# Attention followed by a gated MLP on one Trainium2 core: every second high half of batches three and four on ScalarE, five slots for the probabilities' halves, one bias tile kept in SBUF instead of two

## The chip, the cores and the metric

The kernel runs on one core of a Trainium2 chip. The metric is the device time of one execution in microseconds (us), and less is better. A profile of one execution comes with it; its span runs from the first to the last instruction of the core.

## The reference

Four batches of 576 tokens go through attention with 8 heads of 64, whose scores get a bias that a small MLP makes from relative positions and that all batches share. The 2304 x 512 result then goes through two matrix products with a gated activation between them.

```python
scores = scale * np.matmul(q, k.transpose(0, 1, 3, 2))          # (4, 8, 576, 576)
x = (psi_rel / psi_i)[..., None]                                # from log1p of positions
h = np.maximum(x @ w1 + b1, 0.0)                                # hidden 32
bias = h @ w2                                                   # one value per head
scores = scores + bias.transpose(2, 0, 1)[None, :, :, :]
attn = softmax(scores)                                          # max subtracted, 1e-9 in the divisor
y = np.matmul(attn, v)                                          # back to (2304, 512)
h = y @ w_in                                                    # 512 -> 2048
g = h * np.clip(h + 3.0, 0.0, 6.0) / 6.0
out = g @ w_out                                                 # 2048 -> 512
```

## The kernel before

Numbers that need more than 16 bits are carried as a high and a low float16 half, and a product is summed from three half products. In the code batches count from 0, so that batches three and four of the title are `b` = 2 and `b` = 3.

**Tiles of the attention.** `tiles` lists 144 tiles in order: 4 batches x 4 pairs of heads (`p`) x 9 tiles (`t`) of 128 rows of scores x 576 columns. One tile goes through a fixed pipeline, one stage behind the other:

- `qk_step` (L465): scores on TensorE into a PSUM bank `s_ps`.
- `soft_max` (L477): VectorE adds the bias tile `bt`, keeps the row minimum of the negated sum in `sm` and writes the sum to `bt`.
- `soft_exp` (L485): ScalarE takes the exponential in place and sums the rows.
- `soft_norm` (L491, L499): VectorE takes the reciprocal of the row sum. Then `high_part` writes the **high half** of the scaled probabilities into the first half of a new tile `hl` (128 x 1152 float16): on GpSimd (POOL) at L104, or on ScalarE (ACT) at L110. `hl_mode` reads which one from the configuration: `hl0` for batch one, `hl1` for batch two, `hl` for the batches after, as a string of letters (P POOL, A ACT) that is indexed by the tile's number.
- `soft_low` (L127): VectorE computes the **low half** from `bt` and the high half.
- `soft_turn` (L555): SyncE (SP) issues a DMA that transposes the whole `hl` into the tile `at`. After that the slot of `hl` is free.
- `pv_step` (L630): TensorE multiplies nine transposed chunks with the values' halves; `x_high` (L647, ACT) and `x_low` (L127, VectorE) store the result as halves in `x`.

Most tiles of batch one ("direct", letter F in the configuration) skip the halves and are transposed on TensorE in float32 (L538), so that 118 of the 144 tiles use `hl`.

**Slots.** `hl` comes from a pool of three slots. `bias_out` uses the same slots under the name `bo` (L816): in the first 150 us it evacuates 36 groups of the bias table from PSUM on ACT and SP writes them to DRAM (L818). `load_bias` (L419, L424) later reads bias tiles back from DRAM through SP's queue, two DMAs a tile, each tile being used by two tiles of scores. The bias tiles that `KEEP` lists by (pair, tile) are read once in batch one into a constant tile `kb` and never again.

**The MLP.** `ffn(b, u)` is a generator for half a batch: L705 makes hidden rows `h_ps`, L695, L688, L682 and L684 turn them into the halves `g` (ACT, VectorE, ACT, POOL), L731 multiplies with the second weights and L741 evacuates to `ot`. Its steps are handed out between tiles of the attention by the loop over `n` at the end, so that TensorE has MLP work while a tile waits. What the attention does not take along is done after it.

**The order** of instructions on each engine is not the order of the code: a scheduler places them by priorities and by a timeline that it models for itself, and which includes waits for slots. So a change of a pool's size can move instructions in places that do not use the pool.

Of the kernel before, what the change touches and what calls it, by code (L numbers as in the profile page):

```python
# [24 lines left out]
NG = S // 16  # L25
CQ = 2.0 ** -25
VC = 5 * 128
CFG = {'bw': 0, 'z0': 'ADDD', 'gz': 6, 'zeng': 'AD', 'evac': 'A', 'sg': 'P', 'wm1': 'A', 'wm2': 'A', 'hl1': 'AP', 'ql1': 'PP', 'ql': 'PP', 'gl0': 'PP', 'gl': 'PP', 'hl': 'P', 'vm': 'A', 'g0': 16, 'rwi': 3.0, 'rw0': 0.2, 'rw1': 1.3, 'rb': 1.4, 'rb1': 1.0, 'ro': 3.0, 'rf0': 1.2, 'rf': 1.78, 'rf1': 1.0, 'ch': 1, 'pa': [0, 0, 20], 'la': 6, 'z1': 'AD', 'gz2': 28, 'gq': 2, 'wu': 8, 'act': '', 'tv': 'AAD', 'pf': [0, 0, 0], 'pw': 0, 'po': 0, 'pb': 0, 'sw': 4, 'nb': 0, 'nb1': 0, 'f': 'FFFFFFDD', 'hl0': 'P'}
F64_BIAS = 2.0 ** -112
F64_MAX = float(np.uint32(0x0FEFFFFF).view(np.float32))  # L30

# [2 lines left out]
def attention_moe_kernel(  # L34
# [17 lines left out]
    nc = tc.nc  # L52
    cfg = CFG
    tc.cur_priority = 10000
# [10 lines left out]
    st_p = ctx.enter_context(tc.tile_pool(name="st", bufs=2))  # L65
    v_p = ctx.enter_context(tc.tile_pool(name="v", bufs=2))
    b_p = ctx.enter_context(tc.tile_pool(name="b", bufs=4))
    hl_p = ctx.enter_context(tc.tile_pool(name="hl", bufs=3))
    sm_p = ctx.enter_context(tc.tile_pool(name="sm", bufs=6))
    dr_p = ctx.enter_context(tc.tile_pool(name="dr", bufs=1, space=bass.MemoryType.DRAM))  # L70
    pools = {}
# [332 lines left out]

    bt_t = {}

    KEEP = [(1, 1), (3, 1)]
    kept = {}

    def load_bias(b, p, i):  # L410
        out = b_p.tile([128, 2 * S], F32, tag="bt", name="bt")
        t = out
        if (p, i) in KEEP:
            if b:
# [713 lines left out]
```

## Time and profile before

| | |
|---|---|
| Median of 3 runs | 767.28 us (765.88 to 770.45) |
| Profiled execution, own time | 768.73 us |
| its span | 766.8 us |
| its mean granted TensorE clock | 0.973 |

The span is the profile's own time axis. 768.73 - 766.8 = 1.9 us of the profiled execution's time lie around the span. TensorE's rows are PE (matmuls) and PEld (weight loads); DVE is VectorE, SPq the queue of SyncE. In a row of a timeline the bracket gives the idle time of the engine before the instruction and what ended it.

### The profile page before, as it was taken

The page shows a single profiled execution, that of the slowest core. Times are in us where ns is not written, and L with a number is a line of the kernel's source. Part 1 is how long each engine was busy: PE and PEld are TensorE (multiplying, and loading weights), DVE is VectorE, ACT ScalarE, POOL GpSimd, SP SyncE. Part 2 cuts the span into 40 slices and gives each one's busy share as a digit, 9 for nine tenths or more (in the row PEclk, how much of TensorE's full clock was granted, in tenths as well). Part 3 has the DMA queues.
Part 4 walks back from the last instruction along what each step waited for, and adds up shares of the span by engine and source line. Part 5 has one row for each costly group of instructions (what it writes and reads, how often), then busy time and mean ns, then how long its engine had stood idle before and what let it go on. Part 6 is the DMA issues. An engine that isn't in the chain of part 4 may idle for free.

```text
span 766.8 us, 15078 instructions
## 1 busy us (share of the span) xinstructions
PE 693.5 (90%) x5340; PEld 482.9 (63%) x5340; DVE 509.3 (66%) x1307; ACT 451.8 (59%) x911; POOL 293.8 (38%) x348
## 2 busy tenths in 40 slices
PE   6667788899888888999789999999999999999998
PEld 2223334566567765666576777667877766588775
DVE  7997999998888558876678568746866672030210
ACT  5897999778567358755566366436743661161530
POOL 4111111127564127524576267616652460041320
PEclk9877899999999999999999999999999999999999
DMA  8999767387999999999999998899788642000000
GB/s 256 363 304 285 217 182 233 115 250 219 254 233 224 197 219 215 237 219 259 180 247 224 220 253 150 212 166 220 161 168 172 116 77 64 11 7 22 8 10 27
DMA packets 179275, 137.98 MB, mean 180 GB/s; under 512 B 145920, under 2 KB 152064, under 8 KB 179200
## 3 DMA queue, kind: packets, MB, share of 16 engines
q1 hardware_dynamic: 174592, 132.30, 72.8%
q10 hardware_dynamic: 4608, 4.72, 2.4%
q8 instruction: 42, 0.69, 0.4%
q14 instruction: 33, 0.27, 0.1%
HBM read 84.78 MB, written 15.34 MB: 131 GB/s over the span
## 4 chain that ended last, share of the span: by engine, by line
PE 39%; DMA 13%; DVE 10%; issue 6%; POOL 4%; ACT 3%; SPq 2%; POOLq 0%; ACTq 0%; DVEq 0%
PE o_ps L731 17%; PE h_ps L705 14%; DMA at<-hl 7%; PE pv_ps L630 5%; PE s_ps L465 3%; DVE hl L127 3%; DMA va<-in_vp_dram 3%; DVE bt L477 2%; POOL hl L104 2%; DMA bt<-bias 2%; POOL kl L368 1%; DVE t L688 1%; SPq L419 1%; ACT bt L485 1%; DVE vparts L158 1%
## 5 line engine op out<-in xcount | busy, mean ns | idle before, releaser
L731 PE MATMUL o_ps<-g,wo 128*128 128x256 f16 (+1 forms) x1536 | 227.6, 289 | 5.1 <-ACT ot L741 3.4
L705 PE MATMUL h_ps<-x,wi 128*128 128x256 f16 (+1 forms) x1536 | 218.1, 288 | 7.5 <-DVE t L688 4.7
L731 PEld LDWEIGHTS <-wo 128*128 128x128 f16 x1536 | 146.2, 98 | 59.5 <-issue 7.5
L705 PEld LDWEIGHTS <-wi 128*128 128x128 f16 x1536 | 146.1, 98 | 55.8 <-issue 10.5
L485 ACT ACTIVATE bt<-bt,sm 128x576 f32<-128x576 f32 x144 | 111.1, 771 | 102.0 <-DVE sm L477 87.9
L127 DVE SCALAR_TENSOR_TENSOR hl<-bt,sm,hl 128x576 f16<-128x576 f32 x118 | 120.9, 1029 | 58.9 <-POOL hl L104 51.8
L684 POOL TENSOR_TENSOR g<-t,g 128x256 f16<-128x256 f32 (+1 forms) x128 | 105.4, 832 | 122.0 <-ACT g L682 114.4
L104 POOL TENSOR_SCALAR hl<-bt,sm 128x576 f16<-128x576 f32 x100 | 78.2, 784 | 151.4 <-DMA at<-hl 54.1
L477 DVE CUSTOM_DVE_ANT_0 bt<-s_ps,bt 128x576 f32<-128x576 f32 x128 | 95.1, 748 | 11.0 <-PE s_ps L465 6.2
L688 DVE SCALAR_TENSOR_TENSOR t<-t,t,h_ps 128x320 f32<-128x320 f32 (+1 forms) x112 | 57.2, 513 | 61.5 <-ACT t L695 60.8
L795 PE MATMUL b_ps<-z,w_sb 128*32 128x288 f32 x576 | 67.5, 486 | 28.7 <-ACT z L783 17.9
L682 ACT ACTIVATE g<-t 128x256 f16<-128x256 f32 (+1 forms) x128 | 55.2, 435 | 38.6 <-DVE t L688 38.3
L228 POOL TENSOR_SCALAR w<-w 128x512 f32<-128x512 f32 x32 | 23.0, 718 | 138.6 <-ACT cu L226 118.3
L695 ACT ACTIVATE t<-h_ps,t,hr 128x320 f32<-128x320 f32 (+1 forms) x112 | 65.2, 586 | 18.4 <-PE h_ps L705 12.0
L630 PE MATMUL pv_ps<-at,vh 128*64 128x256 f16 (+1 forms) x468 | 65.7, 296 | 4.8 <-DMA at<-hl 4.6
L795 PEld LDWEIGHTS b_ps<-z,w_sb 128*32 128x32 f32 x576 | 23.6, 121 | 65.8 <-ACT z L783 31.6
L465 PE MATMUL s_ps<-qkh 128*128 128x288 f32 x192 | 53.2, 353 | 7.6 <-DVE sm L477 3.6
L783 ACT ACTIVATE z<-T,bp 128x576 f32<-128x576 f32 x66 | 48.1, 770 | 11.2 <-PE b_ps L795 6.6
L465 PE MATMUL s_ps<-kl,qkh 128*128 128x288 f32 x192 | 50.3, 332 | 0.0
L741 ACT ACTIVATE ot<-o_ps,os 128x256 f32<-128x256 f32 (+1 forms) x32 | 15.8, 494 | 58.2 <-PE o_ps L731 58.1
L630 PEld LDWEIGHTS <-vh 128*64 128x64 f16 x468 | 31.4, 108 | 29.1 <-issue 8.0
L465 PE MATMUL s_ps<-k0t,q0t 128*128 128x288 f32 x144 | 45.6, 443 | 4.3 <-DVE sm L477 2.6
(110 smaller groups left out, 855.2 us busy)
## 6 DMA issues: line engine op xcount, KB each, us to landing
bt<-bias SPq DMA_DIRECT2D x112, 288.0 KB, 4.6
st<-in_qk_dram SPq DMA_DIRECT2D x24, 576.0 KB, 4.7
bias<-bo SPq DMA_DIRECT2D x36, 288.0 KB, 4.6
w<-in_w_in_dram SPq DMA_DIRECT2D x16, 512.0 KB, 7.1
w<-in_w_out_dram SPq DMA_DIRECT2D x16, 512.0 KB, 4.8
vs<-in_vp_dram SPq DMA_DIRECT2D x20, 320.0 KB, 3.7
va<-in_vp_dram SPq DMA_DIRECT2D x16, 320.0 KB, 4.9
bt<-bias SPq DMA_DIRECT2D x32, 144.0 KB, 3.7
```

The costliest lines, as they stand in the source:

```text
L104: nc.gpsimd.tensor_scalar(out=out, in0=full, scalar1=scale, scalar2=1.0, op0=ALU.mult, op1=ALU.mult)
L127: nc.vector.scalar_tensor_tensor(out=out, in0=full, scalar=scale, in1=high, op0=ALU.mult, op1=ALU.subtract)
L465: nc.tensor.matmul(out=ps[:, a, 0:HALF], lhsT=w, rhs=m[:, a * HALF:(a + 1) * HALF], start=(k == 0), stop=(k == len(ops) - 1),)
L477: nc.vector.tensor_tensor_reduce(out=halves(bt), in0=ps, in1=halves(src), op0=ALU.add, op1=ALU.min, scale=-0.125, scalar=3.0e38, accum_out ...
L485: nc.scalar.activation(out=bt, in_=bt, func=AF.Exp, scale=-1.0, bias=sm[:, 0:1], accum_out=sm[:, 1:2])
L630: nc.tensor.matmul(out=ps[64 * s:64 * s + 64, 0:n], lhsT=w[:, 128 * c + 64 * s:128 * c + 64 * s + 64], rhs=at[:, c, s * n:(s + 1) * n], st ...
L684: e.tensor_sub(out=g[:, 1], in0=uu, in1=g[:, 0])
L688: nc.vector.scalar_tensor_tensor(out=t_t[f], in0=t_t[f], scalar=cols(f)[2], in1=h_t.pop(f)[:, 0:n], op0=ALU.min, op1=ALU.mult,)
L695: nc.scalar.activation(out=t_t[f], in_=h_t[f][:, 0:n], func=AF.Relu, scale=cols(f)[0], bias=cols(f)[1],)
L705: nc.tensor.matmul(out=h_t[f][:, 0:n], lhsT=wi[:, a, c, f * 128:(f + 1) * 128], rhs=x[:, e, c], start=(k == 0), stop=(k == 3 * KC - 1),)
L731: nc.tensor.matmul(out=ops[:, 0:n], lhsT=wo[:, a, f, e * 128:(e + 1) * 128], rhs=g_t[f][:, r], start=(f == 0 and a == 0 and r == 0), stop= ...
L795: nc.tensor.matmul(out=pss[a][32 * k:32 * k + 32, 0:HALF], lhsT=w2_sb, rhs=z[:, a * HALF:(a + 1) * HALF],)
```

## The change

Three edits:

- `'hl': 'P'` becomes `'hl': 'AP'`: in batches three and four the high half of tiles with an even number goes to ACT (L110), that of the others stays on POOL (L104). Batch two has had `AP` (`hl1`) before and after.
- The pool of `hl` and `bo` has five slots instead of three.
- `KEEP` loses (3, 1): this bias tile is read from DRAM into `bt` in every batch, like the tiles that were never kept. A kept tile takes 128 x 1152 float32, 4608 bytes a partition, and two slots of `hl` take as much.

```diff
-CFG = {... 'gl': 'PP', 'hl': 'P', 'vm': 'A', ...}
+CFG = {... 'gl': 'PP', 'hl': 'AP', 'vm': 'A', ...}
...
-    hl_p = ctx.enter_context(tc.tile_pool(name="hl", bufs=3))
+    hl_p = ctx.enter_context(tc.tile_pool(name="hl", bufs=5))
...
-    KEEP = [(1, 1), (3, 1)]
+    KEEP = [(1, 1)]
```

What this makes of the order, first on ACT, in batch three, around the evacuations of the MLP's output `ot`. In the kernel before (`bt` the exponential, `tq` a part of the next head's queries, `x` the attention's result):

```order
L741 ACTIVATE ot<-o_ps,os_4404 128x256
L742 DMA out_dram<-ot 128x256
L485 ACTIVATE bt,sm<-bt,sm 128x576
L378 ACTIVATE tq_111<-qkh 128x64
L647 ACTIVATE x<-pv_ps,xr 128x256
L378 ACTIVATE tq_112<-qkh 128x64
L485 ACTIVATE bt,sm<-bt,sm 128x576 x2
```

In the changed kernel, at the same place:

```order
L485 ACTIVATE bt,sm<-bt,sm 128x576 x2
L110 ACTIVATE hl<-bt,sm 128x576
L741 ACTIVATE ot<-o_ps,os_4405 128x256
L647 ACTIVATE x<-pv_ps,xr 128x256
L742 DMA out_dram<-ot 128x256
L485 ACTIVATE bt,sm<-bt,sm 128x576 x2
L741 ACTIVATE ot<-o_ps,os_4405 128x256
L110 ACTIVATE hl<-bt,sm 128x576
```

A high half now stands between the exponentials, once for every two of them; 54 stand on ACT instead of 18 and 64 on POOL instead of 100.

Second, SP's queue at the last pair of heads of batch two. Before (`bias_97` to `bias_105` are the nine parts of the bias table, two for a bias tile):

```order
L419 DMA bt<-bias_97 64x1152
L419 DMA bt<-bias_98 64x1152
L555 DMA_TRANSPOSE at<-hl 128x9x128 x3
L354 DMA st<-in_qk_dram 128x1152
L419 DMA bt<-bias_101 64x1152
```

With the change:

```order
L419 DMA bt<-bias_97 64x1152
L419 DMA bt<-bias_98 64x1152
L555 DMA_TRANSPOSE at<-hl 128x9x128 x2
L419 DMA bt<-bias_99 64x1152
L419 DMA bt<-bias_100 64x1152
L555 DMA_TRANSPOSE at<-hl 128x9x128 x2
```

Two loads of a bias tile stand where none stood; the same holds for batches three and four, six loads in all. On TensorE the order of the 4884 matmuls differs in 634 places, all of them in the first 70% of the order.

## Rows read from the trace of the kernel before

**Rows 1.** Stretches: us, busy us (instructions) of PE PEld DVE ACT POOL, PEclk, DMA share, GB/s.

```profile
0.00:100.00 100.00, 69.52 (x466) 27.94 (x467) 89.73 (x224) 78.53 (x121) 18.59 (x34) 0.83 0.90 284
100.00:200.00 100.00, 88.73 (x668) 56.65 (x668) 92.70 (x283) 84.43 (x163) 31.89 (x38) 1.00 0.69 199
200.00:250.00 50.00, 39.67 (x318) 32.47 (x318) 41.98 (x112) 32.08 (x70) 27.48 (x31) 0.97 1.03 239
250.00:300.00 50.00, 45.94 (x372) 34.56 (x370) 32.18 (x77) 28.45 (x59) 18.19 (x19) 0.97 1.01 206
300.00:350.00 50.00, 45.59 (x334) 30.81 (x331) 38.55 (x100) 33.75 (x69) 22.11 (x24) 1.00 1.14 231
350.00:400.00 50.00, 42.41 (x373) 34.76 (x372) 33.88 (x86) 27.45 (x65) 27.91 (x31) 1.00 1.03 230
400.00:450.00 50.00, 48.57 (x396) 36.62 (x396) 34.11 (x84) 24.12 (x54) 21.64 (x28) 1.00 1.06 224
450.00:700.00 250.00, 249.64 (x1939) 181.59 (x1938) 137.37 (x329) 123.23 (x275) 113.30 (x130) 1.00 0.62 128
```

**Rows 2.** The chain that ended last, 244 to 262 us: start, us, what.

```profile
246.00 7.74 DMA at<-hl
...
253.92 0.76 POOL hl L104
...
254.70 0.83 DVE hl L127
...
255.55 3.25 DMA at<-hl
```

**Rows 3.** Line L555 from 200 to 450 us: who waited for the transposes (us, times).

```profile
  POOL hl L104: 46.5, 12
  ACT hl L110: 13.0, 6
...
DMA to landing us min/median/max: 3.2/4.7/10.0
```

**Rows 4.** TensorE's timeline: matmuls after idle time, start, us, engine, line.

```profile
249.65 0.60 PE L731 MATMUL o_ps<-g,wo 128*128 128x256 f16 x4 [3.44 <-ACT ot L741]
...
261.16 1.03 PE L731 MATMUL o_ps<-g,wo 128*128 128x256 f16 x8 [1.63 <-DVE x L127]
...
306.35 1.41 PE L630 MATMUL pv_ps<-at,vh 128*64 128x320 f16 x18 [1.42 <-DMA at<-hl]
...
367.78 1.41 PE L630 MATMUL pv_ps<-at,vh 128*64 128x320 f16 x18 [3.18 <-DMA at<-hl]
...
381.27 0.37 PE L465 MATMUL s_ps<-qkh 128*128 128x288 f32 x1 [2.37 <-DVE sm L499]
...
387.23 1.03 PE L705 MATMUL h_ps<-x,wi 128*128 128x256 f16 x8 [1.55 <-DVE x L127]
```

**Rows 5.** The tile hl: count, ns min/median/max, first and last start.

```profile
L104 POOL TENSOR_SCALAR hl<-bt,sm x100: 737/744/1427, 181.3 to 636.6; 128x576 f16<-128x576 f32 x100
L110 ACT ACTIVATE hl<-bt,sm x18: 757/775/777, 226.6 to 348.3; 128x576 f16<-128x576 f32 x18
```

**Rows 6.** Timeline from 310 to 313 us: POOL and two low halves.

```profile
310.91 0.82 DVE L127 SCALAR_TENSOR_TENSOR hl<-bt,sm,hl 128x576 f16<-128x576 f32 x1 [1.04 <-ACT hl L110]
...
312.31 0.79 POOL L684 TENSOR_TENSOR g<-t,g 128x320 f16<-128x320 f32 x1
...
312.38 1.34 DVE L127 SCALAR_TENSOR_TENSOR hl<-bt,sm,hl 128x576 f16<-128x576 f32 x1 [0.36 <-POOL hl L104]
```

**Rows 7.** DMA issues: KB each, median us to landing.

```profile
bt<-bias SPq DMA_DIRECT2D x112, 288.0 KB, 4.6
```

**Rows 8.** VectorE's timeline: two readings of the kept bias tile.

```profile
327.84 0.74 DVE L477 CUSTOM_DVE_ANT_0 bt<-s_ps,kb 128x576 f32<-128x576 f32 x1
...
462.08 0.74 DVE L477 CUSTOM_DVE_ANT_0 bt<-s_ps,kb 128x576 f32<-128x576 f32 x1
```

**Rows 9.** ACT's timeline: the one wait of bo for a slot.

```profile
65.37 0.83 ACT L816 ACTIVATE bo<-b_ps,cv_sb,isc 128x576 f32<-128x576 f32 x1 [1.61 <-DMA bias<-bo]
```

More of the change, by code (lines that the diff above doesn't have):

```diff
@@ L27 @@
 VC = 5 * 128
-CFG = {'bw': 0, 'z0': 'ADDD', 'gz': 6, 'zeng': 'AD', 'evac': 'A', 'sg': 'P', 'wm1': 'A', 'wm2': 'A', 'hl1': 'AP', 'ql1': 'PP', 'ql': 'PP', 'gl0': 'PP', 'gl': 'PP', 'hl': 'P', 'vm': 'A', 'g0': 16, 'rwi': 3.0, 'rw0': 0.2, 'rw1': 1.3, 'rb': 1.4, 'rb1': 1.0, 'ro': 3.0, 'rf0': 1.2, 'rf': 1.78, 'rf1': 1.0, 'ch': 1, 'pa': [0, 0, 20], 'la': 6, 'z1': 'AD', 'gz2': 28, 'gq': 2, 'wu': 8, 'act': '', 'tv': 'AAD', 'pf': [0, 0, 0], 'pw': 0, 'po': 0, 'pb': 0, 'sw': 4, 'nb': 0, 'nb1': 0, 'f': 'FFFFFFDD', 'hl0': 'P'}
+CFG = {'bw': 0, 'z0': 'ADDD', 'gz': 6, 'zeng': 'AD', 'evac': 'A', 'sg': 'P', 'wm1': 'A', 'wm2': 'A', 'hl1': 'AP', 'ql1': 'PP', 'ql': 'PP', 'gl0': 'PP', 'gl': 'PP', 'hl': 'AP', 'vm': 'A', 'g0': 16, 'rwi': 3.0, 'rw0': 0.2, 'rw1': 1.3, 'rb': 1.4, 'rb1': 1.0, 'ro': 3.0, 'rf0': 1.2, 'rf': 1.78, 'rf1': 1.0, 'ch': 1, 'pa': [0, 0, 20], 'la': 6, 'z1': 'AD', 'gz2': 28, 'gq': 2, 'wu': 8, 'act': '', 'tv': 'AAD', 'pf': [0, 0, 0], 'pw': 0, 'po': 0, 'pb': 0, 'sw': 4, 'nb': 0, 'nb1': 0, 'f': 'FFFFFFDD', 'hl0': 'P'}
 F64_BIAS = 2.0 ** -112
```

## The prediction, made before the changed kernel had run

> **What bounds the kernel now.** I read stretches first, since shares over the span mix stages. The reader should compare PE's busy time with the length of each stretch [rows 1]. From 450 to 700 us PE is idle for 0.36 us in 250, and what is left after that is MLP work alone: what happens there on ACT, POOL or SP moves nothing, as long as PE's work is the same. Before that PE is idle for 30.5 us in the first 100, 11.3 in the next 100, and 10.3 + 4.1 + 4.4 + 7.6 + 1.4 = 27.8 us between 200 and 450. As PE's work doesn't change, a gain can only come out of these idle times, and out of stretches at the lower clock (0.97 from 200 to 300, 0.83 in the first 100).
>
> From 0 to 200 DVE is busy for 182 of 200 us and ACT for 163: this is the bias table and the preparation of weights, and the pool of `hl` serves it only as `bo`. From 200 to 450 no engine but PE is near full: DVE is busy for 42 of the first 50 us and for 39 and less after, ACT for at most 34, POOL for 28. There the chain of waits is the view to read [rows 2]: a transpose holds a slot for 7.74 us, POOL's next high half starts right after it, DVE's low half follows, the next transpose starts. That is a ring through a pool with too few slots. Line L555's view gives its size [rows 3]: producers of high halves waited 46.5 + 13.0 = 59.5 us for transposes between 200 and 450, 18 times. Most of that costs nothing, because PE has MLP work meanwhile.
>
> So the third view is PE's own gaps, over 1 us each [rows 4], and what stands behind each:
>
> - 3.44 us at 246, for ACT's evacuation `ot`. ACT had waited there for a bias tile, not for a slot.
> - 1.63 us, for `x`, which on DVE is queued behind low halves that came late out of the ring of rows 2.
> - 1.42 and 3.18 us, for the transposes themselves.
> - 2.37 and 1.55 us in batch three. DVE stood behind a low half whose high half came late from POOL, which was working off `kl`, `qkh` and `g` in between.
>
> The DMA engines' share is 1.0 to 1.14 from 200 to 450 [rows 1]: they are the second thing that is nearly full there, and this matters for the rivals.
>
> **The change part by part.**
>
> *Two more slots.* They remove the wait of a high half for the third last transpose. The gap that comes out of the ring goes as a whole: 1.63. The two waits for transposes (1.42 + 3.18 = 4.60) go only as far as the transposes were issued late. A transpose takes 3.2 to 10.0 us to land [rows 3], and at the DMA share of that stretch a transpose that is issued earlier also waits longer. Bounds 0 and 4.60; I take half, 2.3. Sum 3.9.
>
> *Half of the high halves to ACT.* 118 tiles have 100 highs on POOL and 18 on ACT now; 72 belong to batches three and four, and 36 of these move. POOL gets 36 x 0.744 = 26.8 us free, ACT gets 36 x 0.775 = 27.9 us more [rows 5], over about 285 us. Its cover is ACT's idle time: 100 - 51.6 = 48 us from 350 to 450 alone, and after 450 PE never waits. Without that cover it would cost the 27.9. On ACT the exponentials of the next tiles and the MLP's L695 are queued behind a high half that waits for its reciprocal; PE waits for those only through `s_ps` and `h_ps`, which have buffers. What it brings is the two gaps in batch three, where the high half stood behind POOL's other work: 2.37 + 1.55 = 3.9. Bounds 0 (it now stands behind ACT's work) and 3.9; I take 3.9, since ACT is idle for half of that stretch.
>
> *Less meeting of POOL and DVE.* A low half took 0.82 us beside an idle POOL and 1.34 beside L684 on POOL [rows 6]: 0.52 more. If each moved high had met one, DVE would win 36 x 0.52 = 18.7 us; but DVE is busy for 68 of 100 us from 350 to 450, so I count it at nothing, its idle time being the cover.
>
> *One kept bias tile fewer.* Six loads of 288 KB through SP's queue are added, two in each of batches two to four. The tile was read at 328 and 462 us and once more in batch four [rows 8], so that one pair of loads falls into the stretch where PE still has gaps, one just past its end and one well behind it. At the 231 GB/s of that stretch a pair (590 KB) is 2.55 us of all DMA engines. Behind it on SP's queue stand transposes and the next bias tile, for which `soft_max` waits. Bounds: 0, where the queue has a pause, and 2 x 2.55 = 5.1, where both pairs delay PE fully; I take half a pair, +1.3, because PE's gaps there are mostly not for bias tiles. The Trainium skill (DMA: Bandwidth & Descriptors, "Specifications") gives about 358 GB/s as what one core gets from HBM. By that figure a pair would be an estimated 1.65 us, half a pair 0.8, and the sum below would be 0.5 us less; the trace moved 231 GB/s with its DMA engines at a share of 1.14, so that the row's rate stands.
>
> *The bias table's slots.* `bo` waited for a slot once, 1.61 us [rows 9]. PE is idle there anyway, waiting for ACT and DVE, which set the pace. Bounds: -1.6, and +1.6 for order that moved the other way; I take -0.8. The kept tile's two loads of batch one stay two, as those of an ordinary tile.
>
> *Sum.* 768.73 - 3.9 - 3.9 + 1.3 - 0.8 = 761.4 us of the profiled execution's own time. That execution is 1.45 us above the median of 767.28, so the median goes to **760.0 us**, 1.0% less. A measurement of this kernel can tell about 0.5% from no change, that is 763.4 to 771.1 us.
>
> **The rivals.**
>
> *DMA takes the place of the slots (no change).* With five slots the transposes are issued as fast as DVE finishes low halves, and then wait in the DMA queues. For it: the share of 1.0 to 1.14 [rows 1], the 10 us landing [rows 3], which is behind the largest gap for transposes. Against it: from 450 on the attention goes on at a share of 0.62 in the mean. Then the gaps of 1.42 and 3.18 and 1.63 stay, one batch-three gap goes, loads cost 1.3: 767.28 - 2.4 + 1.3 = 766 us. The Trainium skill (Perfetto Trace Analysis, "Identifying the Most-Contended Engine") holds that busy time of the DMA engines misleads because there are 16 of them, and wants HBM traffic as the measure. By that rule the 206 to 239 GB/s of that stretch, below the 284 of the first 100 us [rows 1], would leave room, and this rival would have about 0.1, the rest going to the forecast. The trace agrees as to the traffic; but the same rows show the share of the engines above 1, and the rule leaves out the small packets of the transposes. From the rows alone I give this rival 0.23.
>
> *The added loads delay bias tiles (slower).* This is one mechanism at one place: SP's queue at the last pair of heads. If the loads stand in front of transposes that PE waits for, both pairs cost their full 5.1 us, and nothing else closes because the queue is the bound: 767.28 + 5.1 = 772.4 us. It decides if the landing of `bt<-bias`, 4.6 us now [rows 7], rises to where `soft_max` waits for it in most tiles. Against it: the loads are 6 beside 112. 0.11.
>
> *The whole stretch fills (much faster).* If slots are what keeps 200 to 450 from running as 450 to 650 does, more than the named gaps closes. 27.8 us less the 10.3 of the stretch from 200 to 250, which hold the wait for `ot` and the end of batch one's own kind of tiles, leaves 17.5; with the loads' 1.3 that is 767.28 - 16.2 = 751.1. 0.13.
>
> **How the numbers follow.** The forecast has 0.53, spread about 760 by its own bounds: without the 2.3 and half of the 3.9 it is 764. So 0.10 of it falls within 0.5% of no change. Faster: 0.43 + 0.13 = 0.56; same: 0.23 + 0.10 = 0.33; slower: 0.11. The range of 749 to 768.5 holds the forecast, the rival of no change and most of the large gain, and leaves out the slower one.
>
> **What would show it.** Right: the chain from 200 to 450 has no POOL high right behind a transpose, "POOL hl" and "ACT hl" under L555 fall from 59.5 to under 15 us, PE is idle for about 19 us instead of 27.8 in that stretch, and from 450 on it is as full as before. 54 highs stand on ACT. Wrong: the waits under L555 fall but PE's idle time doesn't, with landings of transposes longer than a median of 4.7 (no change), or bias tiles that land late and `soft_max` idle before them (slower). If the first 200 us differ by more than 2 us, the reordering there has a price that I put too low.

## The result, and the profile of the changed kernel

The changed kernel takes 760.97 us (median of 14 executions, 756.42 to 765.36) beside 767.63 us for the kernel before (14 executions, 765.7 to 770.74): a ratio of 0.9913, 95% interval 0.9894 to 0.9931. That is 6.7 us less. 760.0 had been forecast, and "faster" with 0.56.

The profiled execution took 764.36 us with a span of 762.3 us, so it lies 3.4 us above its median, and its mean granted clock, 0.966, is below the 0.973 of the 14 executions together. It is 4.4 us shorter than the profiled execution before, and what it shows of the clock must be read with this in mind.

The stretches of the changed kernel, with the columns of [rows 1] (busy time of PE, PEld, DVE, ACT, POOL, then the granted clock, the DMA engines' share and GB/s):

```profile
0.00:100.00 100.00, 68.67 (x489) 28.29 (x490) 87.60 (x218) 79.08 (x123) 19.24 (x34) 0.88 0.87 272
100.00:200.00 100.00, 92.29 (x647) 57.50 (x647) 94.90 (x285) 82.64 (x158) 34.05 (x37) 0.98 0.72 210
200.00:250.00 50.00, 41.06 (x312) 34.23 (x312) 43.31 (x119) 31.93 (x71) 29.37 (x33) 0.90 1.05 233
250.00:300.00 50.00, 43.68 (x356) 32.88 (x353) 27.06 (x66) 26.93 (x56) 16.52 (x19) 0.93 1.02 211
300.00:350.00 50.00, 46.43 (x340) 33.11 (x338) 41.79 (x108) 35.19 (x73) 22.62 (x24) 0.93 1.09 221
350.00:400.00 50.00, 50.00 (x397) 37.42 (x397) 35.19 (x95) 34.48 (x76) 22.92 (x26) 1.00 1.17 251
400.00:450.00 50.00, 49.74 (x409) 37.36 (x407) 33.78 (x82) 30.27 (x64) 19.91 (x22) 1.00 1.14 240
450.00:700.00 250.00, 250.00 (x1962) 183.29 (x1961) 131.53 (x324) 135.85 (x293) 87.56 (x105) 1.00 0.62 131
```

PE's idle time is the length of a stretch less PE's busy time. From 200 to 450 us it is 8.9 + 6.3 + 3.6 + 0 + 0.3 = 19.1 us, before 27.8; about 19 had been forecast. But look at where it went. From 350 to 450 it fell from 9.0 to 0.3 us: batch three became as full as what follows it. From 200 to 350 it is 18.8 us before and after. The clock of those three stretches fell from 0.97, 0.97, 1.00 [rows 1] to 0.90, 0.93, 0.93, that is, more of PE's work there ran at the lower of its two levels, 1.2 GHz. In the first 200 us PE was idle for 41.8 us and now for 39.0. A second profile of the changed kernel (e9_again below) agrees on the gaps, 19.5 us from 200 to 350 and 0.7 from 350 to 450, but not on the clock (0.90, 0.97, 0.97) nor on the first 200 us (42.5 us idle): those differ from execution to execution.

Line L555 from 200 to 450 us, which answers to [rows 3] (who waited for the transposes, us and times):

```profile
  ACT hl L110: 4.7, 3
  POOL hl L104: 4.2, 3
  PE pv_ps L630: 2.7, 1
...
DMA to landing us min/median/max: 3.2/5.2/8.7
```

The producers of high halves waited 59.5 us in 18 places before and wait 8.9 us in 6 now (19.7 us in 7 in the second profile). The tile `hl`, with counts as in [rows 5] (ns min/median/max), and below it what its engines waited for:

```profile
L104 POOL TENSOR_SCALAR hl<-bt,sm x64: 738/745/1318, 179.6 to 631.7; 128x576 f16<-128x576 f32 x64
L110 ACT ACTIVATE hl<-bt,sm x54: 758/766/777, 215.6 to 627.1; 128x576 f16<-128x576 f32 x54
...
  DMA at<-hl: 13.5, 7
```

54 high halves stand on ACT, at the same 0.77 us each. What is left of PE's gaps over 1.5 us between 250 and 450 us, in PE's timeline (the bracket is the idle time before and what ended it):

```profile
256.11 7.59 PE L731 MATMUL o_ps<-g,wo 128*128 128x256 f16 x46 [4.75 <-ACT ot L741]
...
289.70 0.31 PE L705 MATMUL h_ps<-x,wi 128*128 128x320 f16 x1 [1.56 <-DVE x L127]
...
310.14 2.31 PE L630 MATMUL pv_ps<-at,vh 128*64 128x320 f16 x15 [2.69 <-DMA at<-hl]
```

Of the gaps in [rows 4] the 1.63 at 260 us, the 3.18 at 365, and the 2.37 and 1.55 of batch three have no counterpart any more. The 1.42 for a transpose has one of 2.69, and the 3.44 for `ot` grew to 4.75. The chain of waits of the changed kernel, 244 to 262 us, tells why `ot` comes late (start, us, what):

```profile
242.79 4.18 DMA at<-hl
...
248.38 7.11 DMA out_dram<-ot
...
255.58 0.48 ACT ot L741
...
256.11 5.96 PE o_ps L731 x31
```

Where the ring of transposes stood in [rows 2], the chain now runs through the store of `ot` to DRAM: 7.11 us until the only buffer of `ot` comes free. So the place of the old ring is now held by another pool with too few buffers; whether removing that wait brings time is tested below.

### The profile page after: what moved, and what is told of

Its sections match the earlier page's. It is cut to its first block, busy times and chain, and to the rows that moved or that the text cites. A ratio compares the mean times of both kernels' runs of the same rounds, so it can differ in the third digit from the quotient of the medians.

```text
span 762.3 us, 15055 instructions
## 1 busy us (share of the span) xinstructions
PE 700.9 (92%) x5340; PEld 487.6 (64%) x5340; DVE 503.9 (66%) x1307; ACT 475.7 (62%) x947; POOL 264.8 (35%) x312
## 3 DMA queue, kind: packets, MB, share of 16 engines
q10 hardware_dynamic: 4608, 4.72, 2.0%
## 4 chain that ended last, share of the span: by engine, by line
PE 57%; DMA 8%; DVE 6%; issue 2%; SPq 2%; ACT 1%; POOL 1%; DVEq 0%; POOLq 0%; ACTq 0%
PE o_ps L731 23%; PE h_ps L705 20%; PE pv_ps L630 8%; PE s_ps L465 6%; DMA va<-in_vp_dram 3%; DMA at<-hl 3%; DVE hl L127 2%; DVE bt L477 1%; DMA out_dram<-ot 1%; SPq L555 1%; DMA bt<-bias 1%; DVE t L688 1%; DVE vparts L158 1%; DVE g L720 1%; SPq L419 1%
## 5 line engine op out<-in xcount | busy, mean ns | idle before, releaser
L731 PE MATMUL o_ps<-g,wo 128*128 128x256 f16 (+1 forms) x1536 | 230.4, 290 | 4.8 <-ACT ot L741 4.8
L684 POOL TENSOR_TENSOR g<-t,g 128x256 f16<-128x256 f32 (+1 forms) x128 | 100.9, 795 | 152.1 <-ACT g L682 146.2
L127 DVE SCALAR_TENSOR_TENSOR hl<-bt,sm,hl 128x576 f16<-128x576 f32 x118 | 115.4, 986 | 30.2 <-ACT hl L110 15.3
L477 DVE CUSTOM_DVE_ANT_0 bt<-s_ps,bt 128x576 f32<-128x576 f32 x136 | 101.5, 750 | 18.4 <-PE s_ps L465 12.7
L104 POOL TENSOR_SCALAR hl<-bt,sm 128x576 f16<-128x576 f32 x64 | 51.3, 803 | 117.5 <-DVE sm L499 74.4
L228 POOL TENSOR_SCALAR w<-w 128x512 f32<-128x512 f32 x32 | 25.3, 791 | 136.6 <-ACT cu L226 122.2
L630 PE MATMUL pv_ps<-at,vh 128*64 128x256 f16 (+1 forms) x468 | 68.4, 303 | 3.8 <-DMA at<-hl 2.7
L741 ACT ACTIVATE ot<-o_ps,os 128x256 f32<-128x256 f32 (+1 forms) x32 | 15.9, 497 | 66.9 <-PE o_ps L731 59.5
```

Of the source, the lines that this page charges most:

```text
L127: nc.vector.scalar_tensor_tensor(out=out, in0=full, scalar=scale, in1=high, op0=ALU.mult, op1=ALU.subtract)
L477: nc.vector.tensor_tensor_reduce(out=halves(bt), in0=ps, in1=halves(src), op0=ALU.add, op1=ALU.min, scale=-0.125, scalar=3.0e38, accum_out ...
L630: nc.tensor.matmul(out=ps[64 * s:64 * s + 64, 0:n], lhsT=w[:, 128 * c + 64 * s:128 * c + 64 * s + 64], rhs=at[:, c, s * n:(s + 1) * n], st ...
L684: e.tensor_sub(out=g[:, 1], in0=uu, in1=g[:, 0])
L731: nc.tensor.matmul(out=ops[:, 0:n], lhsT=wo[:, a, f, e * 128:(e + 1) * 128], rhs=g_t[f][:, r], start=(f == 0 and a == 0 and r == 0), stop= ...
```

## The experiments

Runs that stand in one group share their executions of the kernel before.

| run | slots of hl | highs of batches 3, 4 | kept tiles | other | median us | ratio | 95% interval |
|---|---|---|---|---|---|---|---|
| e1_slots | 5 | POOL | (1,1) | | 763.97 | 0.9954 | 0.9928 to 0.9980 |
| e2_act | 3 | ACT, POOL | both | | 767.25 | 0.9988 | 0.9969 to 1.0008 |
| e3_keep | 3 | POOL | (1,1) | | 769.68 | 1.0010 | 0.9986 to 1.0033 |
| e4_act_keep | 3 | ACT, POOL | (1,1) | | 767.14 | 0.9996 | 0.9969 to 1.0024 |
| e6_four | 4 | ACT, POOL | (1,1) | | 762.94 | 0.9922 | 0.9895 to 0.9949 |
| e7_seven | 7 | ACT, POOL | none | | 769.44 | 1.0006 | 0.9979 to 1.0033 |
| e8_allact | 5 | ACT | (1,1) | | 766.60 | 0.9968 | 0.9938 to 0.9998 |
| e11_ot2 | 5 | ACT, POOL | (1,1) | two buffers for ot | 768.70 | 0.9982 | 0.9955 to 1.0009 |
| e9_again | 5 | ACT, POOL | (1,1) | the change itself | 761.92 | 0.9892 | 0.9863 to 0.9921 |
| e10_keep0 | 5 | ACT, POOL | none | | 769.20 | 1.0005 | 0.9979 to 1.0031 |
| e11_bo_own | 5 | ACT, POOL | none | bo in two slots of its own | 765.01 | 0.9952 | 0.9930 to 0.9973 |
| e12_act_queue | 5 | ACT, POOL | (1,1) | bias loads on ACT's queue | 803.06 | 1.0392 | 1.0342 to 1.0442 |

The first four form one group, the next four and the last four two more. Differences between two runs below are those of their ratios, times 768 us; where two intervals enter, I add their half widths as squares. A single execution of one kernel can lie 5 to 9 us beside its median, so a profile's stage lengths are good to a few us only.

**The parts alone.** The edits are the diff's own lines, each put back or taken alone: e1_slots has `'hl': 'P'`, e2_act has `bufs=3` and `KEEP = [(1, 1), (3, 1)]`, e3_keep both `'hl': 'P'` and `bufs=3`, e4_act_keep `bufs=3`. For e1_slots, against the change:

```diff
-CFG = {... 'hl': 'AP', ...}
+CFG = {... 'hl': 'P', ...}
```

> The change without its first edit: five slots and one kept bias tile, high halves of batches three and four all on POOL. If the slots do the work, this takes 760 to 762 us (ratio about 0.992) like the whole change, and the waits of high halves for transposes between 200 and 450 us stay under 15 us. If both edits bring about half each, as forecast, it takes 764 to 765 us (0.995 to 0.997): the gap behind the ring of slots closes, those of batch three stay at 2 to 4 us. If ACT's share does the work, 767 us or a little more.

> The first edit alone: every second high half of batches three and four on ACT, three slots, two kept tiles. If the slots do the work, 767 us (ratio 0.998 to 1.002), and POOL and ACT together still wait some 60 us for transposes between 200 and 450 us. If both edits bring half each, 763 to 764 us (0.995). If ACT's share does the work, 760 to 762 us.

> The third edit alone: one kept tile, three slots, high halves on POOL. Six loads are added and nothing else. By the forecast +0 to +2.5 us (ratio 1.000 to 1.003). By the theory that loads delay bias tiles on SP's queue, +5 us (1.007) and more time of soft_max waiting for bias tiles. If the order alone makes a difference, up to 3 us in either direction, with the difference in the first 200 us.

> First and third edit without the slots: every second high half on ACT, one kept tile, three slots. If the slots are needed for any gain, this takes 767 to 770 us (ratio 1.000 to 1.003). If ACT's share brings half by itself, 764 to 766 us. If ACT's share does everything, 761 us.

The loads of one more tile (e3_keep) cost +0.10% with a half width of 0.23%: +0.8 us, not told from nothing. The two slots are e1_slots against e3_keep: -0.56% with 0.35%, that is -4.3 us. Half of the high halves on ACT bring -0.14% with 0.36% where there are three slots (e4_act_keep against e3_keep; e2_act alone -0.12% with 0.20%), and -0.41% with 0.32% where there are five (the change against e1_slots), -3.1 us. So the slots bring a gain that is clear of the noise by themselves; ACT's part is clear of it only beside five slots. That it is worth less beside three is not shown: the two figures differ by 0.27% with a half width of 0.48%. What would speak for it is line L555 of e4_act_keep, 200 to 450 us:

```profile
  POOL hl L104: 32.5, 10
  ACT hl L110: 24.0, 14
...
  PE pv_ps L630: 5.3, 4
DMA to landing us min/median/max: 3.3/5.1/8.3
```

56.5 us of waits for slots, nearly the 59.5 of [rows 3]: with three slots the waits went along with the high halves, from POOL (46.5 to 32.5 us) to ACT (13.0 to 24.0). On the other hand e1_slots, whose high halves are all on POOL, fills the end of the stretch by itself. Its windows:

```profile
300.00:350.00 50.00, 44.44 (x331) 31.55 (x330) 40.34 (x105) 33.49 (x71) 22.56 (x25) 0.97 1.06 237
350.00:400.00 50.00, 50.00 (x387) 36.48 (x387) 35.32 (x91) 30.38 (x67) 28.78 (x31) 1.00 1.13 243
400.00:450.00 50.00, 50.00 (x415) 38.34 (x414) 36.52 (x88) 24.91 (x57) 24.16 (x28) 1.00 1.10 242
```

PE is not idle at all from 350 to 450 there. The batch-three gaps of 2.37 and 1.55 us, which the prediction gave to ACT's part, are gone without it. From 200 to 350 PE is idle for 25.6 us in that kernel and for 18.8 with ACT's part too; but the first high half that the edit moves stands at 356 us, so this difference can only come from a new order of the instructions or from the spread of single executions. (The profiled execution of e1_slots took 772.57 us, 8.6 us more than the kernel's median.)

Why the slots alone can close these gaps is to be seen in POOL's timeline of the kernel before, ahead of the gap of 2.37 us at 381:

```profile
377.73 0.74 POOL L104 TENSOR_SCALAR hl<-bt,sm 128x576 f16<-128x576 f32 x1 [3.20 <-PE s_ps L465]
378.44 1.40 POOL L368 TENSOR_TENSOR kl<-st,qkh 128x576 fp32r<-128x576 f32 x1
```

POOL had not been working off `kl` and `qkh` before this high half: it had been idle for 3.20 us, and they came behind it. The row names `s_ps` as what ended the wait, but in the trace's semaphore records POOL waited for a transpose that SP issued at 372.06 and that had landed by 377.48, that is, for a slot. Only the high half before the gap of 1.55 us, at 384.79, stands behind `kl` and `qkh`.

**How many slots, and how much ACT.**

```diff
-    hl_p = ctx.enter_context(tc.tile_pool(name="hl", bufs=5))
+    hl_p = ctx.enter_context(tc.tile_pool(name="hl", bufs=4))
```

> The change with four slots instead of five. Slots 3, 4, 5 at the same other edits: three gave a ratio of 0.9996, five 0.9913. If a high half's wait for the third last transpose was nearly short enough, four do as well as five: 761 to 762 us, waits of high halves for transposes under 25 us. If each slot brings its part, 764 us (0.995). If five are needed for the ring to vanish, 766 us.

e7_seven has `bufs=7` and `KEEP = []`, e8_allact `'hl': 'A'`.

> Seven slots, no kept bias tile, first edit as in the change. If the ring of slots has vanished with five, two more bring nothing, and six more loads cost at most 2.5 us: 761 to 764 us (ratio 0.991 to 0.995). If slots still bind in batch two, 756 to 759 us. If the DMA queues are what is left, seven slots only lengthen the landing of transposes, from a median of 5.2 us between 200 and 450 us to over 5.5, and the time is 761 to 765 us.

> The change with every high half of batches three and four on ACT instead of every second, so that POOL has none there. If POOL's other work before a high half is what costs, this is as good as the change or up to 2 us better: 759 to 761 us. If the two engines working side by side is what helps, ACT's queue is now what DVE waits for: 763 to 766 us, and low halves wait longer for ACT than the 15.3 us in the change's profile.

Four slots give 0.9922, not told from the 0.9913 of five. Yet line L555 of the kernel with four shows, 200 to 450 us:

```profile
  POOL hl L104: 27.3, 7
  ACT hl L110: 15.4, 9
```

42.7 us of waits, against 8.9 and 19.7 in the two profiles with five, in the same time. With seven slots there is one wait, and no gain is left at all:

```profile
  POOL hl L104: 6.2, 1
  PE pv_ps L630: 3.1, 4
...
DMA to landing us min/median/max: 3.3/5.2/9.9
```

So the sum of the waits for slots is no measure of the time: it was 59.5 (before), 42.7, 8.9 and 6.2 us (seven slots) for 767.6, 762.9, 761.0 and 769.4 us. All high halves on ACT (e8_allact) is slower than every second one by 0.55% with 0.35%. From 200 to 450 us low halves waited 13.2 us for ACT there and 9.9 in the change. Its PE timeline has, in batch three, a gap that the change has not:

```profile
399.53 1.47 PE L705 MATMUL h_ps<-x,wi 128*128 128x256 f16 x12 [3.94 <-DVE t L688]
```

That half of them is the better choice is shown for these two kernels; that it is this gap which costs the 4 us is only likely.

**The next pool that is too small.** 

```diff
-            ot = f_p.tile([128, gw], F32, tag="o", bufs=1 if first else 2, name="ot")[:, 0:n]
+            ot = f_p.tile([128, gw], F32, tag="o", bufs=2, name="ot")[:, 0:n]
```

> The change, and two buffers instead of one for the output tile ot in the first half of batch one's MLP. In the change's profile ACT waits 7.23 us at 248 us for the DMA that empties the only ot, and TensorE 4.75 us for ACT, with 6.8 us at the lower clock after it. If that wait recurs in most executions, this takes 755 to 758 us (ratio 0.983 to 0.988). If it is a chance meeting with a full DMA queue in that one execution, 760 to 761 us. If the freed stretch only moves the wait to the transposes, 759 to 760 us.

The wait for `ot` is gone, and the time is 768.7 us: 0.69% with 0.33% *more* than the change, or 5.3 us, so that one more buffer cost most of the gain. None of the three expectations allowed for that. PE's timeline in that kernel at the same place, and later:

```profile
258.25 3.97 PE L731 MATMUL o_ps<-g,wo 128*128 128x256 f16 x21 [3.82 <-DVE x L127]
...
334.95 0.74 PE L630 MATMUL pv_ps<-at,vh 128*64 128x320 f16 x3 [3.76 <-DMA at<-hl]
```

The gap of 4.75 us became one of 3.82 at the same matmul, for `x`, and a new one of 3.76 opened. A gap that is named in the profile needn't be won when its releaser is removed: the one that came second is close behind it, and the order changes as well. Which of the two cost the 5.3 us was not separated.

**The change again, and no kept tile.** e9_again is the change itself. e10_keep0:

```diff
-    KEEP = [(1, 1)]
+    KEEP = []
```

and e11_bo_own on top of that:

```diff
-        t = hl_p.tile([128, S], F32, tag="hl", name="bo")
+        t = pools["e"].tile([128, S], F32, tag="bo", bufs=2, name="bo")
```

> The changed kernel once more, beside the three others and the kernel before. If the gain is the kernel's and not the chip's, the ratio to the kernel before falls into 0.989 to 0.993 again (about 761 us). If chips or single executions decide it, as the spread of 756 to 765 us among its executions allows, it lies at 0.995 or above.

> The changed kernel with no kept bias tile at all: the last kept tile is loaded in every batch as well, six more loads of 288 KB. Five slots as in the change. Theory of the prediction (a pair of loads costs half its transfer where the stretch up to 450 us takes it, nothing behind): +1.3 us on the changed kernel, 762 to 763 us. Rival one (loads are free, SP's queue has pauses): 761 us. Rival two (the first kept tile is read early, where SP's queue has no pause; this, and not the order, lost the gain in the run with seven slots, which kept no tile either): 767 to 769 us.

> As the kernel without kept tiles, and in addition the bias table's bo in two slots of its own, so that it gets nothing of the five slots. If the change's gain has nothing to do with bo (its first exponential came 8 us earlier, but the end of batch one only 1 us), the time is that of the kernel without kept tiles within 0.5%, and the first exponential comes about 8 us later again, as in the kernel before, with the end of batch one within 2 us. If the earlier start of the attention is what the five slots bring, it is 3 to 4 us slower than the kernel without kept tiles, and the end of batch one moves by as much.

The change repeats at 0.9892, in another group of runs: its gain is the kernel's. Without the last kept tile all of it is lost (+1.13% with 0.39%, 8.7 us by the ratios, 7.3 by the medians). That is the time which rival two of that expectation gave; its reason, the loads "and not the order", is not shown. It is also what seven slots lost, since e7_seven kept no tile either and has the same ratio; two slots beyond five bring nothing there. Line L555 of e10_keep0, 200 to 450 us, and two rows of its PE timeline:

```profile
  POOL hl L104: 20.1, 4
  ACT hl L110: 7.3, 2
  PE pv_ps L630: 5.9, 4
...
DMA to landing us min/median/max: 3.3/5.4/9.8
```

```profile
312.13 2.34 PE L630 MATMUL pv_ps<-at,vh 128*64 128x320 f16 x15 [3.81 <-DMA at<-hl]
...
342.51 1.41 PE L630 MATMUL pv_ps<-at,vh 128*64 128x320 f16 x18 [1.60 <-DMA at<-hl]
```

That fits loads which stand between the transposes. But batch one, where a kept tile is loaded too and so nothing is added, ended at 221.2 us there (I take the 37th exponential, the first after the 36 of batch one) against 213.6 and 216.9 in the two profiles of the change. So part of the loss may be the order that the scheduler found, and how much can't be told from these runs.

e11_bo_own, with the same loads, starts its first exponential at 71.4 us instead of 59.8, ends batch one at 223.8 instead of 221.2, and is 0.53% (half width 0.34%) *faster* than e10_keep0. So an early start of the attention is not what the five slots bring. In the change, too, the first exponential came at 58.1 instead of 66.1 us, and batch one ended at 213.6 instead of 214.7: seven of the eight us were given back.

**SP's queue.** In the changed kernel, SP issues during most of batch three, with loads between the transposes. Here they go to ACT's queue:

```diff
-CFG = {... 'act': '', ...}
+CFG = {... 'act': 'b', ...}
```

> The changed kernel with the loads of bias tiles issued from ACT's queue instead of SP's. SP's queue issues for 45 of 50 us from 350 to 450 in the changed kernel, and the loads are in it between the transposes. If SP's queue is what is left between 200 and 350 us, where the change closed nothing (18.8 us idle before and after), the waits for transposes there shrink and the time falls by 2 to 4 us, to 757 to 759 us. Rival: a load on ACT's queue stands behind ACT's waits for slots of bt and before high halves and exponentials; then exponentials come late and the time is 763 us or more. If neither queue matters, it is 761 us within 0.5%.

803 us: on the rival's side, and far beyond it. The timelines of that kernel at 338 to 362 us, SP's, ACT's, PE's and PEld's rows:

```profile
344.99 18.69 SPq L555 DMA_TRANSPOSE at<-hl  x5
...
351.99 0.78 ACT L110 ACTIVATE hl<-bt,sm 128x576 f16<-128x576 f32 x1 [3.03 <-DMA st<-in_qk_dram]
...
358.45 3.47 ACTq L419 DMA_DIRECT2D bt<-bias  x2
...
358.40 0.48 PE L630 MATMUL pv_ps<-at,vh 128*64 128x320 f16 x1 [7.79 <-DMA bt<-bias]
...
358.40 0.13 PEld L630 LDWEIGHTS <-vh 128*64 128x64 f16 x1 [8.12 <-DMA at<-hl]
```

Relieved of the loads, SP's queue took 18.69 us to issue five transposes, 3.7 us each. In the change, two took 3.83 us with loads on both sides of them:

```profile
341.09 1.23 SPq L419 DMA_DIRECT2D bt<-bias  x2
342.37 3.83 SPq L555 DMA_TRANSPOSE at<-hl  x2
346.32 1.72 SPq L419 DMA_DIRECT2D bt<-bias  x2
```

So here SP's queue was not long because of the loads in it: from 200 to 450 us the issue of a transpose took 2.4 us in the mean instead of 2.0, and 8.75 at the longest instead of 4.37, though its median fell from 1.96 to 1.77. PE's wait of 7.79 us is for a transpose: PE's row names a bias load, but this matmul reads `at` and `vh` and no bias tile, PEld's row names the transpose, and the one issued at 344.99 landed at 358.36. From 200 to 450 us the high halves waited 72.9 us for slots again (8.9 in the change), and `soft_max` 14.9 us for bias tiles (2.2), which is the rival's side of it. Which of the two costs how much was not separated.

## Why the prediction was right, and where not

The time (760.0 forecast, 761.0 measured) and the sign hold. That the sum came so near is in part luck: each of its two large terms is known to 2.5 us or worse, the gaps that closed were not all the ones it named, and edits as small as a buffer for `ot` or a place for `bo` moved the time by 4 to 5 us. Point by point:

- **What bounds it.** Right: all gain lies before 450 us. In the profiled executions PE's idle time fell by 2.8 us before 200, 8.7 from 200 to 450 and 0.4 from 450 to 700. The sum, 11.9, is more than the 4.4 us between the two profiles, since PE's busy time rose from 693.5 to 700.9 us: the changed kernel's profile has 53 us at the lower clock, the one before 44, and at half the clock those 9 us more explain, by an estimate, at most 4.5 of the 7.4 us. The list of gaps "over 1 us each" was not whole: it has six, 13.6 us, and PE's timeline from 200 to 450 us shows seven more, 10.9 us (2.93 at 219 the longest). From 200 to 350 us nothing closed in sum.
- **Two more slots, -3.9.** Measured -4.3 with 2.7. The size is right, the place is not. In the change 1.42 + 3.18 became 2.69, about the half that was forecast; but with the slots alone PE still waited 4.4 us for transposes in two places, and what closed there are the gaps of batch three. That other gaps made up the same sum is luck.
- **Half of the highs to ACT, -3.9.** Measured -3.1 with 2.5 beside five slots, but -1.1 with 2.8 beside three. The step that failed is "What it brings is the two gaps in batch three, where the high half stood behind POOL's other work": these gaps close with the slots alone, since the high half before the first of them waited for a slot and not for POOL's other work (3.20 us, above). So the sum gave to ACT what the slots bring. By which gap ACT pays was not settled: in the profiles PE's idle time from 200 to 700 us differs between e1_slots and the change by 6.8 us before 350, where no high half had moved, and by 0.6 after.
- **Loads, +1.3.** Measured +0.8 with 1.8 for this tile. The rule behind it (half a pair's transfer in the stretch that still has gaps) did not carry over to the other tile: by it, e10_keep0 should have lost 1.3 to 2.6 us, and it lost 7.3, of which the order may have a part.
- **Less meeting of POOL and DVE, nothing.** DVE's busy time over the first 700 us fell from 500.5 to 495.2 us, and PE is full where it fell most, behind 450 us (137.4 to 131.5): rightly counted at nothing.
- **bo's slots, -0.8.** The end of batch one came 1.1 us earlier, within the bounds of 1.6. But e11_bo_own shows that changing only where `bo` lies can move the whole kernel by 4 us: the bounds were too narrow for that.
- **The ring.** The chain from 200 to 450 has no high half behind a transpose as a piece of length, and waits fell to 8.9 us ("under 15"), in the second profile to 19.7. That this is the sign of the gain was wrong: with four slots 42.7 us of waits remained, and the gain too.
- **The rivals.** That DMA takes the place of the slots: the landing's median rose from 4.7 to 5.2 us and two of the gaps stayed as one of 2.69 us, so it took part of them back between 200 and 350, while from 350 to 450 251 and 240 GB/s went through where it had been 230 and 224. That the whole stretch fills: it did in its last 100 us and not before. That added loads delay bias tiles: not with this tile (`soft_max` waited 3.3 us for them from 200 to 450 before, 1.3 in e3_keep, 2.2 in the change). A rival that the prediction did not have is the order: a gain that comes from where the scheduler put things, and not from the slots. Against it, three kernels with three slots lie at 0.9988 to 1.0010 and the kernels with four and five slots and one kept tile at 0.9892 to 0.9968; for it, the same five slots with a second buffer for `ot` lie at 0.9982 and without a kept tile at 1.0005. No run here holds the order and changes the slots alone, so the share of each stays open.

The Trainium skill (Perfetto Trace Analysis, "Optimization Strategy") says that a gap which keeps recurring on the engine that ought to be full can mean too little memory for the next tile. Here the trace agrees in part: a fourth and fifth slot brought 4.3 us, but the recurring waits were on POOL and ACT, and PE, the fullest engine, had a few gaps of different causes.

## What to carry to other kernels

Count the waits for a pool's slots only where the bounding engine is idle behind them: taking 59.5 us of waits to 42.7 or to 8.9 gave nearly the same time. Before a gap is given to an engine's other work, look whether that engine was busy or idle ahead of it: POOL's 3.20 us of idle time would have given the gap to the slots. Two edits that may serve the same gap are not simply to be added: run each alone and both. Where a scheduler sets the order, an edit changes it in other places too: a buffer for `ot` cost 0.69% and another place for `bo` gained 0.53%, with half widths of 0.33% and 0.34%. How much of either is the order is open, but a term of 3 us is only known when the whole version has run.

## What was not expected of the hardware

- **Transposes and the DMA engines.** In the first 100 us, before any of these transposes, 272 GB/s went at a share of 0.87, or 313 GB/s for a full share; from 350 to 400 us 251 GB/s went at 1.17, or 215. The Trainium skill (Advanced Engine Details and Errata, "X-Bar Transpose (TRN2)") holds that transposing DMAs are as fast as others; with this mix of transposes and loads the rows don't agree. The packets in the trace of the changed kernel tell the two apart: from 200 to 450 us the packets of 256 bytes, of which each transpose makes 1152, moved 80.7 GB/s at a share of 0.54, or 149 for a full share, and the packets of 4608 bytes, bias loads for the most part, 100.0 GB/s at 0.37, or 270. What transposes reach with no other traffic no run here shows.
- **Two queues were not better than one here.** With the bias loads on ACT's queue the median landing of a load rose from 4.7 to 6.0 us and of a transpose from 4.9 to 6.2, and the longest transpose of the stretch landed after 18.2 us instead of 8.7.
- **The clock before the first exponential.** Two executions of the same changed kernel, 764.36 and 767.76 us, differ by 2.9 us before the first exponential (58.1 and 61.0 us) and by little after it. Their granted clocks in the first 61 us were 0.92 and 0.88, the idle times of PE in them 20.0 and 21.1 us. So most of this spread arose where PE is busy for two thirds of the time and the clock goes up and down between its two levels; as the kernel is the same, it is no effect of the change. That the clock causes it is not shown.
